# Attention, feed-forward and routed experts on one core: the first pass's weights converted two pieces a pair over six pairs, R's addition on GpSimd, M_prev in two buffers

## The chip, the core and the metric

The kernel runs on one core of one Trainium2 chip. The metric is device time in microseconds (us). The kernel before takes 1056.38 us (median of three runs, 1054.51 to 1058.94). The trace is of one further execution, which took 1052.92 us.

## The reference

Three layers follow one another. Attention: 4 batches, 8 heads, 576 positions, 64 wide; the causal softmax output is mixed, head by head, with a read from a memory `M_prev`. Feed-forward: 2304 tokens, 512 to 2048 to 512, squared ReLU. Routed experts: 8 experts, 288 tokens each, chosen greedily by sorted logits.

```python
a = np.exp(scores); a /= a.sum(-1, keepdims=True) + 1e-09
local = np.matmul(a, v)
mem_out = (phi(q) @ M_prev) / (phi(q) @ z_prev + 1e-6)
x = g * mem_out + (1 - g) * local          # g = sigmoid(beta)
h = np.maximum(x @ w_in, 0); x = (h * h) @ w_out
...
out[mask] = np.maximum(x[mask] @ w1[e], 0) @ w2[e]
```

`w_in` and `w_out` reach the kernel as 64-bit floats, read as pairs of 32-bit words; everything else is 32-bit.

## The kernel before

The program is attention with the first feed-forward pass woven in, then the rest of the feed-forward layer, then the experts. Only the first part is touched.

Attention works on 16 pairs of heads. `step(n)` runs from n = -2 to 16, and each step carries work of several pairs at once: it transposes the probabilities of pair n (`trans`), computes the scores of pair n+1 (`score`, `exponentials`), reads out pairs n and n-1 (`read`), and prepares the operands of pairs n+1 and n+2. A step has ten parts u; `fill` is called in each of them, at 20 counted places a step. TensorE's instructions stand in the order in which the code is written. On VectorE (DVE), ScalarE (ACT), GpSimd (POOL) and SyncE (SP, which issues the loads and stores), a scheduler sets the order when the program is built; each of these engines then works strictly through its list.

In `exponentials`, ScalarE's exponential leaves row sums in `R[:, 1]`. When it has done u = 3 and u = 8 of a pair's nine blocks of rows, VectorE adds 1e-9 (L243) and takes the reciprocal (L244), and GpSimd multiplies the probabilities `P` by it (L246). TensorE then transposes `P` (L271) and multiplies. That is 32 such additions over 128x4 or 128x5 values.

The feed-forward layer goes over the 16 chunks of the hidden dimension in three passes; the first pass takes chunks 0 to 5, and needs for each chunk a piece of `w_in` and a piece of `w_out`. `Ffn.weights` makes one piece: a load of 512 KB (`raw`, L428), then `narrow`, which rebuilds 32-bit floats from the 64-bit ones (ScalarE L36 writes `r`; VectorE L37, L38, L39 make `gf`), then `split` into two parts (ScalarE L25, GpSimd L26). In this text, a conversion is one such piece. Twelve conversions belong to the first pass. `fill` takes two from the list at every tenth counted place from step 0 on, `w_in` and `w_out` of a chunk in turn: four in each of steps 0, 1 and 2, as far as the scheduler keeps them there. From step 4 on (`n >= HP`), `fill` also weaves in the matmuls of the first pass (`Ffn.first`), about 60 a step.

`load_memory` brings a pair's `M_prev` into one buffer `mraw` and splits it; the next pair's load waits for that. At the start, `og9`, a table of the mixing weights, is built by twelve small copies on VectorE.

Of the kernel before, what the change touches and what calls it, by code (L numbers as in the profile page):

```python
# [29 lines left out]
def narrow(nc, f, tmp, raw):  # L30

    low, high = raw[..., 0], raw[..., 1]
    nc.scalar.activation(tmp.bitcast(F32), high.bitcast(F32), AF.Copy, scale=2.0 ** -112)  # L36
# [12 lines left out]
def attention(tc, ident, q, k, v, M_prev, z_prev, beta, x_d, fill, ended):  # L49
# [5 lines left out]
    with ExitStack() as ctx:  # L55
# [43 lines left out]
        og = one.tile([128, H], F32, name="og")  # L99
        nc.vector.tensor_scalar(og, g, -1.0, 1.0, op0=OP.mult, op1=OP.add)  # L100
        og9 = one.tile([128, HP, 9], F32, name="og9")
        for hp in range(HP):
            nc.vector.tensor_copy(og9[:, hp, 0:8].rearrange("p (t j) -> p t j", j=2),
                                  og[:, None, 2 * hp:2 * hp + 2].to_broadcast([128, 4, 2]))
            for j in range(2):
                nc.vector.tensor_copy(og9[64 * j:64 * j + 64, hp, 8:9],
                                      og[64 * j:64 * j + 64, 2 * hp + j:2 * hp + j + 1])
        qb = [one.tile([128, 2, 128], F32R, name=f"qb{i}") for i in range(2)]
        for t_ in qb:
            nc.vector.tensor_copy(t_.rearrange("p s c -> p (s c)"), maskw[:, 0:256])  # L110
# [6 lines left out]

        def load_memory(n):
            b, hp = divmod(n, HP)
            raw = one.tile([128, 2, 64], F32, name="mraw")  # L120
            for j in range(2):
                nc.sync.dma_start(raw[64 * j:64 * j + 64], M_prev[b, 2 * hp:2 * hp + 2].rearrange("h d e -> d h e"))
            m = MB[n] = two.tile([128, 2, 128], F32R, name="mb")
            split(nc, m[:, :, 0:64], m[:, :, 64:128], raw)
# [98 lines left out]
        def exponentials(n, u, ps):  # L223
# [16 lines left out]
            nc.scalar.activation(pw, pw, AF.Exp, bias=R[:, 0, u:u + 1], scale=-1.0, accum_out=R[:, 1, u:u + 1])  # L240
            if u in (3, 8):
                us = slice(0, 4) if u == 3 else slice(4, 9)
                nc.vector.tensor_scalar(R[:, 2, us], R[:, 1, us], 1e-9, None, op0=OP.add)  # L243
                nc.vector.reciprocal(R[:, 2, us], R[:, 2, us])  # L244
                for w in range(us.start, us.stop):
                    nc.gpsimd.tensor_scalar(PP[n][w], PP[n][w], R[:, 2, w:w + 1], og9[:, hp, w:w + 1],  # L246
                                            op0=OP.mult, op1=OP.mult)
# [145 lines left out]
class Ffn:  # L393
# [19 lines left out]
        nc.vector.tensor_tensor(self.two8, ident[0:16, 0:8], ident[0:16, 8:16], op=OP.add)  # L413
        self.win, self.wout, self.Y, self.have = {}, {}, {}, 0

    def weights(self, c, part, home, pool, eng, psum=None):

        nc = self.nc
        if part == 0:
            a = self.win[c] = home.tile([128, 2, KD, 128], F32R, name="win")  # L420
            dst = a.rearrange("p s k f -> p s (k f)")
            src = self.w_in[:, 256 * c:256 * c + 256].rearrange("(k p) f -> p k f", p=128)
        else:
            dst = self.wout[c] = home.tile([128, 2, DM], F32R, name="wout")
            src = self.w_out[128 * c:128 * c + 128].rearrange("p (k f) -> p k f", k=KD)
        first = pool is self.start
        raw = pool.tile([128, 2 * DM], I32, name=f"raw{part}" if first else "raw")
        nc.sync.dma_start(raw.rearrange("p (k f) -> p k f", k=KD), src)  # L428
        t_ = (psum or self.two).tile([128, DM], I32, name="pr" if psum and psum is self.p2x else "r")
        held = part and c >= PASSES[-1][0]  # L430
        f_ = (self.two if first else self.keep if held else pool).tile([128, DM], I32, name="gf")
        narrow(nc, f_, t_, raw.rearrange("p (n t) -> p n t", t=2))
        split(nc, dst[:, 0], dst[:, 1], f_.bitcast(F32), eng)
        if held:
            self.sums += [(f_, c - PASSES[-1][0], e) for e in range(8)]
        yield
# [713 lines left out]
def tile_attention_ffn_moe(ctx, tc, q, k, v, M_prev, z_prev, beta, w_in, w_out, w_gate, w1, w2, out):  # L1150
# [19 lines left out]
    def chunks(cs, home, pool, psum=None):  # L1170
        for c in cs:
            for part in range(2):
                yield from f.weights(c, part, home, pool, nc.gpsimd, psum)

    sctx = ExitStack()
    f.start = sctx.enter_context(tc.tile_pool(name="ffs", bufs=1, side="right"))
    conv, work = chunks(PASSES[0], wa, f.start), f.first(sctx.enter_context(tc.tile_pool(name="gfirst", bufs=8, side="right")))
    owed = [0, 0]

    def fill(n, c, place=True):  # L1180
        owed[1] += place
        if place and n >= 0 and owed[1] % 10 == 0:
            for _ in range(2):
                next(conv, None)
        owed[0] += c
        while n >= HP and owed[0] > 0:
            e = next(work, 0)
            if not e:
                break
            owed[0] -= e  # L1190
        owed[0] = min(owed[0], 0)
# [84 lines left out]
```

## Time and profile before

| what | us |
|---|---|
| median of three runs | 1056.38 (1054.51 to 1058.94) |
| profiled execution | 1052.92 |
| its span, first to last instruction | 1051.2 |
| attention with the first pass woven in | about 0 to 383 |
| steps 0 to 2 | 21.82 to 104.55 |
| steps 3 to 5 | 104.55 to 169.27 |
| steps 6 on | 169.27 to about 383 |

The steps are cut where TensorE begins the first scores of a pair (L217 on 128 columns). Read the table with the span: the times of stretches count from its start. The 1.7 us that the execution takes beyond its span lie around it.

### The profile page before, as it was taken

The numbers are of one execution on the slowest core, as the hardware profiler recorded it, in microseconds if no ns is written. First come the engines' busy times: TensorE is split into PE (matmuls) and PEld (weight loads), VectorE is DVE, ScalarE is ACT, GpSimd is POOL, SyncE is SP. The second block draws the span as 40 slices with busy tenths as digits, with TensorE's granted clock in tenths as the row PEclk, the third lists the DMA queues.
The fourth block names the chain that finished last, engine by engine and source line by source line (L and its number), as shares of the span: only waits on it lengthen the run. The fifth ranks groups of instructions, "written<-read, shape, count | busy, mean of one in ns | idle before, by whom it ended". The sixth has DMA issues, their size and how long they took to land.

```text
span 1051.2 us, 19788 instructions
## 1 busy us (share of the span) xinstructions
PE 959.6 (91%) x7017; PEld 879.5 (84%) x7017; DVE 666.5 (63%) x1966; ACT 553.2 (53%) x1370; POOL 528.1 (50%) x503
## 2 busy tenths in 40 slices
PE   5667789999999989999999999999598999999996
PEld 4455678988898989999999999977497888989996
DVE  6999878887888737456426952335775577674110
ACT  6676877988888746444322343431152443354531
POOL 3565666566765726334312111211294856687841
PEclk9677899999999999999999999999698999999998
DMA  6354455554645276769584232101541454447400
GB/s 151 103 152 122 95 155 141 125 160 98 174 107 142 68 235 215 226 215 307 196 289 152 86 128 98 61 22 39 203 161 62 168 183 148 153 136 254 150 27 27
DMA packets 150723, 150.75 MB, mean 143 GB/s; under 512 B 71640, under 2 KB 122840, under 8 KB 150496
## 3 DMA queue, kind: packets, MB, share of 16 engines
q1 hardware_dynamic: 147552, 140.05, 43.1%
q0 software_dynamic: 3072, 9.44, 2.9%
q8 instruction: 55, 0.90, 0.3%
q14 instruction: 44, 0.36, 0.1%
HBM read 111.69 MB, written 37.77 MB: 142 GB/s over the span
## 4 chain that ended last, share of the span: by engine, by line
PE 62%; DVE 13%; ACT 9%; issue 7%; DMA 4%; POOL 3%; SPq 2%; POOLq 0%; ACTq 0%; DVEq 0%
PE ph L1054 12%; PE ph L44 7%; PE ph L45 6%; PE ph L46 6%; PE py L44 4%; PE py L45 4%; PE py L46 4%; ACT P L240 3%; POOL wsp L1038 3%; PE ps L312 3%; PE ps L217 2%; PE rs L831 2%; PE ps L271 2%; DMA wraw<-in_moe_w_dram 1%; DVE ptb L26 1%
## 5 line engine op out<-in xcount | busy, mean ns | idle before, releaser
L477 POOL TENSOR_TENSOR gf<-r 128x384 f32<-128x384 f32 (+1 forms) x108 | 87.0, 807 | 205.7 <-ACT r L475 197.6
L1038 POOL TENSOR_TENSOR wsp<-wraw,wsp 128x1024 fp32r<-128x1024 f32 x64 | 151.0, 2393 | 41.5 <-ACT wsp L1036 41.2
L1054 PE MATMUL ph<-xs,wsp 128*128 128x288 f32 x768 | 121.3, 308 | 0.0
L26 DVE TENSOR_TENSOR gs<-gf,gs 128x384 fp32r<-128x384 f32 (+1 forms) x108 | 63.6, 589 | 90.7 <-ACT gs L25 90.4
L1054 PE MATMUL ph<-hs,wsp 128*128 128x288 f32 x768 | 115.9, 304 | 0.0
L246 POOL TENSOR_SCALAR P<-P,R,og 128x128 f32<-128x128 f32 (+2 forms) x144 | 95.4, 675 | 35.6 <-DVE R L244 15.3
L1054 PEld LDWEIGHTS ph<-xs,wsp 128*128 128x128 f32 x768 | 107.8, 194 | 3.5 <-issue 2.8
L1054 PEld LDWEIGHTS ph<-hs,wsp 128*128 128x128 f32 x768 | 105.7, 191 | 0.9 <-DVE hs L1078 0.4
L1036 ACT ACTIVATE wsp<-wraw 128x1024 fp32r<-128x1024 f32 x64 | 64.0, 1052 | 48.2 <-DMA wraw<-in_moe_w_dram 30.8
L475 ACT ACTIVATE r<-ph 128x384 f32<-128x384 f32 (+1 forms) x108 | 48.6, 450 | 75.5 <-PE ph L46 74.4
L240 ACT ACTIVATE P<-P,R 128x128 f32<-128x128 f32 (+2 forms) x144 | 83.3, 580 | 8.6 <-DVE R L228 4.2
L25 ACT ACTIVATE gs<-gf 128x384 fp32r<-128x384 f32 (+1 forms) x108 | 52.5, 486 | 56.3 <-POOL gf L477 48.0
L44 PE MATMUL ph<-xt,win 128*128 128x384 f32 x240 | 81.3, 339 | 0.0
L45 PE MATMUL ph<-xt,win 128*128 128x384 f32 x240 | 80.9, 337 | 0.0
L46 PE MATMUL ph<-xt,win 128*128 128x384 f32 x240 | 80.7, 336 | 0.0
L271 PE MATMUL ps<-ident,P 128*128 128x128 f32 x320 | 62.5, 303 | 13.9 <-DVE ptb L26 4.8
L44 PE MATMUL ph<-xs,win 128*128 128x288 f32 x192 | 63.5, 331 | 3.8 <-ACT yo L514 2.5
L217 PE MATMUL ps<-kt,qt 64*128 64x128 f32 (+3 forms) x384 | 56.3, 390 | 10.0 <-DVE kt L26 3.4
L45 PE MATMUL py<-gs,wout 128*128 128x384 f32 x192 | 64.6, 337 | 0.0
L26 DVE TENSOR_TENSOR ptb<-ps,ptb 128x256 fp32r<-128x256 f32 (+3 forms) x128 | 59.6, 467 | 6.9 <-ACT ptb L25 5.1
L46 PE MATMUL py<-gs,wout 128*128 128x384 f32 x192 | 63.9, 336 | 0.0
L228 DVE CUSTOM_DVE_ANT_0 P<-ps,maskw 128x128 f32<-128x128 f32 (+3 forms) x128 | 58.6, 483 | 7.6 <-PE ps L135 4.1
(259 smaller groups left out, 2612.9 us busy)
## 6 DMA issues: line engine op xcount, KB each, us to landing
wraw<-in_moe_w_dram SPq DMA_DIRECT2D x32, 1024.0 KB, 5.5
xt<-xs_d SPq DMA_DIRECT2D x12, 1536.0 KB, 7.2
x_d<-xo SPq DMA_DIRECT2D x32, 288.0 KB, 3.7
xf<-x_d SPq DMA_DIRECT2D x32, 288.0 KB, 3.7
xs_d<-xs SPq DMA_DIRECT2D x8, 1152.0 KB, 5.9
raw<-in_moe_w_in_dram SPq DMA_DIRECT2D x16, 512.0 KB, 4.8
raw<-in_moe_w_out_dram SPq DMA_DIRECT2D x16, 512.0 KB, 4.8
yp<-yo SPq DMA_DIRECT2D x32, 144.0 KB, 4.0
```

What stands on the lines that cost most here:

```text
L26: (eng or nc.vector).tensor_tensor(lo, src, hi.bitcast(F32), op=OP.subtract)
L44: nc.tensor.matmul(out, lhi, rhi, start=start, stop=False)
L45: nc.tensor.matmul(out, lhi, rlo, start=False, stop=False)
L46: nc.tensor.matmul(out, llo, rhi, start=False, stop=stop)
L217: nc.tensor.matmul(ps[j][:, 0:w], qt[r0, a, qs], kt[r0, b, 0:w], start=i == 0, stop=i == 2)
L240: nc.scalar.activation(pw, pw, AF.Exp, bias=R[:, 0, u:u + 1], scale=-1.0, accum_out=R[:, 1, u:u + 1])
L246: nc.gpsimd.tensor_scalar(PP[n][w], PP[n][w], R[:, 2, w:w + 1], og9[:, hp, w:w + 1], op0=OP.mult, op1=OP.mult)
L271: nc.tensor.transpose(tr[:, 128 * i:128 * i + 128], P[:, 128 * i:128 * i + 128], ident)
L477: nc.gpsimd.tensor_tensor(gf, r, r, op=OP.mult)
L1036: nc.scalar.activation(w[:, 0, hs], raw[:, hs], AF.Copy)
L1038: eng.tensor_tensor(w[:, 1, hs], raw[:, hs], w[:, 0, hs].bitcast(F32), op=OP.subtract)
L1054: nc.tensor.matmul(out, l[a], r[b], start=i + p == 0, stop=i == n - 1 and p == 2)
```

## The change

- The twelve conversions come in another order, all six of `w_in` first, then six of `w_out`, and at other places: one at each of two places in each of steps 0 to 5 (places 10 and 20; in step 5, places 4 and 10).
- `fetch` takes the load out of `weights`; the load of the next piece is issued at the place of the present one. Two buffers, raw0 and raw1, take turns (before there were two as well, one for `w_in` and one for `w_out`).
- These loads, and ScalarE's first operation of each conversion, are kept in the program's order, so the scheduler may not move them ahead.
- R's addition of 1e-9 (32 times) runs on GpSimd; the reciprocal stays on VectorE.
- `mraw` has two buffers; `og9` is built by three copies in place of twelve.

```diff
-        for hp in range(HP):
-            nc.vector.tensor_copy(og9[:, hp, 0:8].rearrange("p (t j) -> p t j", j=2),
-                                  og[:, None, 2 * hp:2 * hp + 2].to_broadcast([128, 4, 2]))
-            for j in range(2):
-                nc.vector.tensor_copy(og9[64 * j:64 * j + 64, hp, 8:9],
-                                      og[64 * j:64 * j + 64, 2 * hp + j:2 * hp + j + 1])
+        pairs = og.rearrange("p (h j) -> p h j", j=2)
+        nc.vector.tensor_copy(og9[:, :, 0:8].rearrange("p h (t j) -> p h t j", j=2),
+                              pairs[:, :, None, :].to_broadcast([128, HP, 4, 2]))
+        for j in range(2):
+            nc.vector.tensor_copy(og9[64 * j:64 * j + 64, :, 8], pairs[64 * j:64 * j + 64, :, j])
...
-            raw = one.tile([128, 2, 64], F32, name="mraw")
+            raw = two.tile([128, 2, 64], F32, name="mraw")
...
-                nc.vector.tensor_scalar(R[:, 2, us], R[:, 1, us], 1e-9, None, op0=OP.add)
+                nc.gpsimd.tensor_scalar(R[:, 2, us], R[:, 1, us], 1e-9, None, op0=OP.add)
...
+CONVERT = {0: (10, 0), 1: (10, 0), 2: (10, 0), 3: (10, 0), 4: (10, 0), 5: (4, 10)}
...
+    def fetch(self, c, part, pool, name="raw"):
+
+        raw = pool.tile([128, 2 * DM], I32, name=name)
...
+        a = self.nc.sync.dma_start(raw.rearrange("p (k f) -> p k f", k=KD), src)
+        if pool is self.start:
+            self.tc.keep_in_program_order(a)
+        return raw
...
-        narrow(nc, f_, t_, raw.rearrange("p (n t) -> p n t", t=2))
+        a = narrow(nc, f_, t_, raw.rearrange("p (n t) -> p n t", t=2))
+        if first:
+            self.tc.keep_in_program_order(a)
...
+    def apart(cs, home, pool):
+        todo = [(part, c) for part in range(2) for c in cs]
+        raws = []
+        for n, (part, c) in enumerate(todo):
+            for part_, c_ in todo[len(raws):n + 2]:
+                raws.append(f.fetch(c_, part_, pool, f"raw{len(raws) % 2}"))
+            yield from f.weights(c, part, home, pool, nc.gpsimd, None, raws[n])
...
-    conv, work = chunks(PASSES[0], wa, f.start), ...
+    conv, work = apart(PASSES[0], wa, f.start), ...
...
-        if place and n >= 0 and owed[1] % 10 == 0:
-            for _ in range(2):
-                next(conv, None)
+        if place and owed[1] % 20 in CONVERT.get(n, ()):
+            next(conv, None)
```

TensorE's order stays as it is, instruction for instruction; the other engines' orders differ as far as the end of attention. Below, three places (lines of the changed kernel are one or more higher: L107 is the old L106).

VectorE near the program's start, where the copies into og9 stand between the first pair's q side (qp) and its k (kt). Before:

```order
L176 SCALAR_TENSOR_TENSOR qp<-nq_175,e 128x640
L103 COPY og_205<-og 128x8
L106 COPY og_205<-og 64x1 x2
L103 COPY og_205<-og 128x8
L106 COPY og_205<-og 64x1 x2
L103 COPY og_205<-og 128x8
L106 COPY og_205<-og 64x1 x2
L103 COPY og_205<-og 128x8
L106 COPY og_205<-og 64x1 x2
L26 TENSOR_TENSOR kt<-ps,kt 128x512
```

With the change:

```order
L176 SCALAR_TENSOR_TENSOR qp<-nq_175,e 128x640
L104 COPY og_205<-og 128x4x8
L107 COPY og_205<-og 64x4 x2
L26 TENSOR_TENSOR kt<-ps,kt 128x512
```

Three copies stand ahead of kt in place of twelve.

VectorE in step 0, from the phi operation of a coming pair (L176) on; L37, L38 and L39 are a conversion's operations, L243 and L244 R's addition and reciprocal. Before:

```order
L176 SCALAR_TENSOR_TENSOR qp<-nq_176,e 128x640
L200 TENSOR_TENSOR qpt_426<-ps,qpt_426 64x512
L39 SCALAR_TENSOR_TENSOR gf<-raw_526,r 128x512
L26 TENSOR_TENSOR pta<-ps,pta 128x256
L244 RECIPROCAL R<-R 128x5
...
L37 TENSOR_SCALAR gf<-r 128x512
L200 TENSOR_TENSOR qpt_426<-ps,qpt_426 64x64
L243 TENSOR_SCALAR R<-R 128x4
L180 TENSOR_REDUCE nr<-e 128x10
L200 TENSOR_TENSOR qpt_427<-ps,qpt_427 64x512
L38 SCALAR_TENSOR_TENSOR r<-r,gf 128x512
```

With the change, from L176 on:

```order
L176 SCALAR_TENSOR_TENSOR qp<-nq_176,e 128x640
L200 TENSOR_TENSOR qpt_417<-ps,qpt_417 64x512
L26 TENSOR_TENSOR pta<-ps,pta 128x256 x2
L26 TENSOR_TENSOR qb_210<-ps,qb_210 64x64
L200 TENSOR_TENSOR qpt_417<-ps,qpt_417 64x64
L26 TENSOR_TENSOR ptb<-ps,ptb 128x3x128
L200 TENSOR_TENSOR qpt_418<-ps,qpt_418 64x512
L200 TENSOR_TENSOR qpt_418<-ps,qpt_418 64x64
L26 TENSOR_TENSOR qt<-ps,qt 128x512
L26 TENSOR_TENSOR kt<-ps,kt 128x512
L37 TENSOR_SCALAR gf<-r 128x512
```

The first conversion of the step begins only behind qt and kt; before, parts of two stand ahead of the reciprocal and among the qpt operations. The addition L243 is gone from this list.

VectorE in step 5, with the change, where before no conversion stood; gs is the feed-forward pass's hidden part, ptb the transposed probabilities:

```order
L184 TENSOR_TENSOR nr<-nr,g 128x10
L37 TENSOR_SCALAR gf<-r 128x512
L38 SCALAR_TENSOR_TENSOR r<-r,gf 128x512
L39 SCALAR_TENSOR_TENSOR gf<-raw_1800,r 128x512
L26 TENSOR_TENSOR gs<-gf,gs 128x288
L26 TENSOR_TENSOR qt<-ps,qt 128x512
L26 TENSOR_TENSOR gs<-gf,gs 128x288
L26 TENSOR_TENSOR kt<-ps,kt 128x512
L37 TENSOR_SCALAR gf<-r 128x512
L26 TENSOR_TENSOR ptb<-ps,ptb 128x3x128
```

A whole conversion stands ahead of gs, qt and kt, and the next one begins right behind them.

## Rows read from the trace of the kernel before

**Rows 1.** Windows by part: us, PE, PEld, DVE, ACT, POOL busy (count), PEclk, DMA share, GB/s

```profile
21.82:104.55 82.73, 56.43 (x288) 45.18 (x288) 77.23 (x198) 60.31 (x169) 48.09 (x48) 0.73 0.47 132
104.55:169.27 64.72, 55.66 (x380) 46.60 (x379) 54.64 (x172) 52.84 (x161) 40.47 (x48) 0.92 0.47 116
169.27:383.00 213.73, 208.47 (x1590) 190.00 (x1589) 172.20 (x526) 172.24 (x523) 130.15 (x157) 1.00 0.50 132
```

**Rows 2.** The same view, steps 2, 3, 4 and 5 one by one

```profile
78.25:104.55 26.30, 18.87 (x101) 14.95 (x100) 24.53 (x61) 18.64 (x53) 15.39 (x16) 0.77 0.43 122
104.55:125.43 20.88, 16.34 (x100) 12.66 (x99) 19.33 (x56) 15.89 (x48) 12.86 (x15) 0.84 0.39 90
125.43:147.95 22.52, 18.32 (x121) 15.14 (x120) 17.11 (x60) 17.96 (x56) 12.75 (x16) 0.92 0.61 163
147.95:169.27 21.32, 20.99 (x161) 18.80 (x160) 18.20 (x58) 18.99 (x59) 14.86 (x18) 1.00 0.39 93
```

**Rows 3.** Windows of VectorE's conversion operations (tile gf), steps 0, 1, 2

```profile
21.82:51.19 29.37, 12.40 (x15) 0.68 0.42 126
51.19:78.25 27.06, 10.57 (x14) 0.75 0.55 148
78.25:104.55 26.30, 8.02 (x9) 0.77 0.43 122
```

**Rows 4.** Tile gf up to 110 us: durations min/median/max in ns, starts

```profile
L37 DVE TENSOR_SCALAR gf<-r x12: 410/482/1727, 23.9 to 94.7; 128x512 int32<-128x512 int32 x12
L38 DVE SCALAR_TENSOR_TENSOR r<-r,gf x12: 673/690/1728, 26.3 to 98.4; 128x512 int32<-128x512 int32 x12
L39 DVE SCALAR_TENSOR_TENSOR gf<-raw,r x12: 675/754/1639, 28.9 to 101.8; 128x512 int32<-128x512 int32 x12
```

**Rows 5.** Windows of R's addition alone (L243, VectorE)

```profile
21.82:104.55 82.73, 4.29 (x6) 0.73 0.47 132
104.55:169.27 64.72, 4.72 (x7) 0.92 0.47 116
169.27:383.00 213.73, 7.02 (x18) 1.00 0.50 132
```

**Rows 6.** R's addition up to 400 us, its durations in ns

```profile
L243 DVE TENSOR_SCALAR R<-R x32: 154/221/2607, 17.6 to 360.5; 128x4 f32<-128x4 f32 x16, 128x5 f32<-128x5 f32 x16
```

**Rows 7.** Timeline of VectorE and TensorE: start, us, engine, line; in brackets idle before

```profile
112.09 2.61 DVE L243 TENSOR_SCALAR R<-R 128x4 f32<-128x4 f32 x1
178.92 1.14 DVE L243 TENSOR_SCALAR R<-R 128x4 f32<-128x4 f32 x1
180.57 0.79 PE L217 MATMUL ps<-kt,qt 64*128 64x384 f32 x6 [1.54 <-DVE ptb L26]
```

**Rows 8.** The same view of four engines at the program's start

```profile
9.39 0.16 DVE L103 COPY og<-og 128x8 f32<-128x8 f32 x1
9.69 1.53 POOL L177 TENSOR_TENSOR e<-qp,zb 128x640 f32<-128x640 f32 x1 [4.97 <-DMA zb<-in_z_prev_dram]
9.77 1.48 DVE L103 COPY og<-og 128x8 f32<-128x8 f32 x1
12.29 0.82 DVE L26 TENSOR_TENSOR kt<-ps,kt 128x512 fp32r<-128x512 f32 x2
13.03 1.43 PE L217 MATMUL ps<-kt,qt 64*128 64x128 f32 x10 [3.44 <-DVE kt L26]
13.87 0.74 ACT L172 ACTIVATE e<-nq 128x640 f32<-128x640 f32 x1 [0.51 <-DMA nq<-in_q_dram]
```

**Rows 9.** Groups by line and shape up to 383 us: busy us, mean ns, idle before

```profile
L36 ACT ACTIVATE r<-raw 128x512 f32<-128x512 f32 x12 | 8.0, 671 | 5.1 <-DMA raw<-in_moe_w_out_dram 2.9 <-DMA raw<-in_moe_w_in_dram 2.1
L246 POOL TENSOR_SCALAR P<-P,R,og 128x128 f32<-128x128 f32 x32 | 15.4, 489 | 8.6 <-DVE R L244 8.0 <-PE ph L46 0.7
L703 POOL IOTA j<- 128x3 f32 x1 | 0.1, 145 | 0.0
```

**Rows 10.** Waits of SP's queue up to 400 us: total us, times, longest

```profile
SPq L122 <- DVE mb L26: 66.0, 9, 14.1
```

More of the change, by code (lines that the diff above doesn't have):

```diff
@@ L35, in narrow @@
     low, high = raw[..., 0], raw[..., 1]
-    nc.scalar.activation(tmp.bitcast(F32), high.bitcast(F32), AF.Copy, scale=2.0 ** -112)
+    a = nc.scalar.activation(tmp.bitcast(F32), high.bitcast(F32), AF.Copy, scale=2.0 ** -112)
     nc.vector.tensor_scalar(f, tmp, 3, None, op0=OP.logical_shift_left)
@@ L39, in narrow @@
     nc.vector.scalar_tensor_tensor(f, low, 29, tmp, op0=OP.logical_shift_right, op1=OP.bitwise_or)
+    return a
 def mm3(nc, out, lhi, llo, rhi, rlo, start, stop):
@@ L414, in __init__, with weights @@
         self.win, self.wout, self.Y, self.have = {}, {}, {}, 0
-    def weights(self, c, part, home, pool, eng, psum=None):
+    def fetch(self, c, part, pool, name="raw"):
+        raw = pool.tile([128, 2 * DM], I32, name=name)
+        if part == 0:
+            src = self.w_in[:, 256 * c:256 * c + 256].rearrange("(k p) f -> p k f", p=128)
+        else:
+            src = self.w_out[128 * c:128 * c + 128].rearrange("p (k f) -> p k f", k=KD)
+        a = self.nc.sync.dma_start(raw.rearrange("p (k f) -> p k f", k=KD), src)
+        if pool is self.start:
+            self.tc.keep_in_program_order(a)
+        return raw
+    def weights(self, c, part, home, pool, eng, psum=None, raw=None):
         nc = self.nc
@@ L421, in weights @@
             dst = a.rearrange("p s k f -> p s (k f)")
-            src = self.w_in[:, 256 * c:256 * c + 256].rearrange("(k p) f -> p k f", p=128)
         else:
             dst = self.wout[c] = home.tile([128, 2, DM], F32R, name="wout")
-            src = self.w_out[128 * c:128 * c + 128].rearrange("p (k f) -> p k f", k=KD)
         first = pool is self.start
-        raw = pool.tile([128, 2 * DM], I32, name=f"raw{part}" if first else "raw")
-        nc.sync.dma_start(raw.rearrange("p (k f) -> p k f", k=KD), src)
+        raw = self.fetch(c, part, pool) if raw is None else raw
         t_ = (psum or self.two).tile([128, DM], I32, name="pr" if psum and psum is self.p2x else "r")
@@ L1173, in chunks @@
                 yield from f.weights(c, part, home, pool, nc.gpsimd, psum)
+    def apart(cs, home, pool):
[5 more added lines that the diff above has]
+            yield from f.weights(c, part, home, pool, nc.gpsimd, None, raws[n])
     sctx = ExitStack()
     f.start = sctx.enter_context(tc.tile_pool(name="ffs", bufs=1, side="right"))
-    conv, work = chunks(PASSES[0], wa, f.start), f.first(sctx.enter_context(tc.tile_pool(name="gfirst", bufs=8, side="right")))
+    conv, work = apart(PASSES[0], wa, f.start), f.first(sctx.enter_context(tc.tile_pool(name="gfirst", bufs=8, side="right")))
     owed = [0, 0]
```

## The prediction

> **What bounds the kernel now.** I read the windows first, cut where TensorE begins a new pair's first scores. In steps 0 to 2 TensorE is busy 56.43 of 82.73 us while VectorE is busy 77.23 us, 93% [rows 1]: VectorE sets the pace there. In steps 3 to 5 VectorE is busy 54.64 of 64.72 us (84%) and TensorE 55.66; from step 6 on TensorE is busy 208.47 of 213.73 us, so only 5.3 us can be won there [rows 1]. The granted clock goes with it: 0.73, 0.92, 1.00 of full speed, so between the levels of 1.2 and 2.4 GHz at first, after idle stretches of TensorE, and at 2.4 GHz from step 5 on [rows 1, 2]. So time can be won up to 169 us; what comes behind attention keeps its work and nearly its order, and I leave it as it is.
>
> Next I asked what fills VectorE in the early steps. Its conversion operations take 12.40, 10.57 and 8.02 us in steps 0, 1 and 2 [rows 3], together 30.99 us for twelve, or 2.58 us each. Undisturbed, one takes 0.410 + 0.673 + 0.675 = 1.76 us by the shortest of its three operations; the longest are 1.73, 1.73 and 1.64 us [rows 4]. Something holds them up. R's addition shows it more plainly: 4 or 5 values a partition take 154 ns at best and 2607 at worst [rows 6]. At 178.92 us one takes 1.14 us, and TensorE then waits 1.54 us for the transposed probabilities behind it [rows 7]. All 32 take 4.29 us in steps 0 to 2 (with 4.72 in steps 3 to 5 and 7.02 later) [rows 5].
>
> Why so long? The copy at 9.77 us takes 1.48 us where its like at 9.39 took 0.16, and GpSimd runs an operation from 9.69 to 11.22 [rows 8]: VectorE's copy ends with GpSimd's operation. The Trainium skill (SBUF — State Buffer, Who interferes with whom) says that certain VectorE operations from SBUF share a port pair with GpSimd, and that the loser of that lock waits for the whole other instruction. The trace agrees, with the 1.48 us.
>
> **The change, term by term.** The sums are made against the profiled 1052.92 us, which lies 3.5 us under the median of 1056.38; I apply the difference to the median.
>
> *Start.* Twelve copies fill VectorE from 9.39 to 12.29 us, and TensorE waits 3.44 us for the kt behind them [rows 8]. Three copies need some 0.5 us, so kt could go at 9.9: 2.4 us won. But ScalarE stands idle until 13.87 for its next e, by the trace for a load (which the change doesn't hasten), and its exponentials are queued behind that; the second or third copy may also still meet GpSimd's operation. Ends: 0 and -2.4; I take the middle, **-1.2**.
>
> *Steps 0 to 2, six conversions fewer and R's additions gone.* By VectorE's load: 77.23 - 30.99 / 2 - 4.29 = 57.4 us, plus the 5.5 us for which it is idle now, is 62.9: 19.8 us won. From the other side, by the nearest step without a conversion: step 3 takes 20.88 us, of which VectorE is busy 19.33 [rows 2]. R's addition in it takes at least the 2.61 us at 112.09 [rows 7]. So 20.88 - 2.61 + 2 x 2.58 = 23.4 us a step with two conversions, 70.3 for three: 12.4 won. Between them: **-16**. Loading a place earlier also removes ScalarE's waits on raw pieces, 5.1 us [rows 9]; I give it nothing, because VectorE is the busier engine throughout and covers it. Were VectorE not the bound, they would be part of the same gain.
>
> *Steps 3 to 5, six conversions more, R's additions gone.* VectorE's load becomes 54.64 - 4.72 + 6 x 2.58 = 65.4 us. If it can be filled to the 93% of the early steps, that needs 65.4 / 0.93 = 70.3 us: 5.6 lost. At the undisturbed 1.76 us it is 60.5 / 0.93 = 65.0: 0.3 lost. Step 4 has slack (17.11 of 22.52 us), step 5 has none on TensorE (20.99 of 21.32) [rows 2]. There a conversion stands whole ahead of gs, qt and kt, and TensorE waits for these. I take **+3.5**, nearer the upper end, as GpSimd is busy 40.47 of 64.72 us here, 63%, against 48.09 of 82.73, 58%, in steps 0 to 2 [rows 1], so the price should not fall.
>
> *Steps 6 on.* R's addition frees 7.02 us of VectorE [rows 5], but TensorE is idle only 5.3 us in all, and 1.5 of it is the wait of rows 7. Ends 0 and -2.5; I take **-1**.
>
> *R's addition on GpSimd.* No row shows GpSimd adding on four columns. From below the index list of three columns, 0.145 us; from above the 128-column multiplication, 0.489 us [rows 9], so 4.6 to 15.6 us on an engine that is busy 48% to 63% of the time: hidden, save in the chain exponential, addition, reciprocal, multiplication, where VectorE's 0.154 is replaced. Thirteen of them lie in the steps up to 5 [rows 5]; at up to 0.34 more each that is 0 to 4.4 us. I take **+1**. Behind a waiting addition stand the multiplications of the same probabilities, which would wait anyway, and at times a feed-forward operation.
>
> *M_prev twice.* SP's queue stands 66.0 us, in nine waits, behind the one mraw [rows 10]; but it loads a pair ahead, and TensorE names no such load in its waits. **0**, with perhaps 1 us won; if the cover were gone, one late load would cost the longest wait, 14.1 us.
>
> Sum: -1.2 - 16 + 3.5 - 1 + 1 = **-13.7 us**, 1039.2 for an execution like the profiled one, **1042.7** against the median.
>
> **The rivals.**
>
> *The late steps pay it back* (0.18). In steps 3 to 5 each conversion meets GpSimd at work in each of its three operations. At the longest of rows 4 one costs 5.09 us; half-way between that and the mean, 3.8 us, six cost 23, VectorE's load is 72.7 and the stretch 78.2 us: +13.5 in place of +3.5, so -3.7 in all, 1052.7. For it: step 5's full TensorE [rows 2]. Against it: in steps 0 to 2, with three operations a conversion, the counts give 2.3 to 2.7 us each [rows 3]. The lock of which the Trainium skill tells (the same page and section) would lead here: by it the price hangs on how often the two engines meet.
>
> *More than the middle* (0.20). VectorE's load decides, and the clock rises earlier because TensorE is less often idle: -19.8 in steps 0 to 2, +0.3 in steps 3 to 5, -2.4 at the start, the rest as above: -21.9, 1034.5. For it: 93% in the early steps. Against it: other chains (ScalarE is busy 60.31 of 82.73 us [rows 1]) should show as VectorE clears.
>
> *Slower: ScalarE waits at the pinned places* (0.07). The loads of raw and L36 can no longer be moved by the scheduler. If SP's queue stands (it does for 14.1 us at worst [rows 10]) when a raw load's turn comes, L36 waits on ScalarE, and behind it all exponentials. At the longest of today's kind of wait, 2.5 us for each of twelve, and with nothing hidden, this costs 30 us: +16, 1072.7. From 13.7 / 12 = 1.1 us a conversion on the kernel is slower than before. Against it: the load is issued ten places, about half a step, ahead, and the M_prev that held SP's queue now has a second buffer.
>
> **How the numbers follow.** The forecast holds 0.55, the rivals 0.18, 0.20 and 0.07. Ends of the terms together: -2.4 - 19.8 + 0.3 - 2.5 + 0 = -24.4, so 1032.0; 0 - 12.4 + 5.6 + 0 + 4.4 = -2.4, so 1054.0. The second rival lies inside, the first just inside; I give 1032 to 1054 for 8 in 10. A measurement of this kernel can tell about 0.5%, 5.3 us, from no change: faster means under 1051.1. Forecast and second rival are nearly all faster, of the first rival about a quarter: 0.79. No change 0.14, slower 0.07.
>
> **What would show it.** Right: in the profile after, steps 0 to 2 take 64 to 69 us, with VectorE's conversion operations near 5 us a step; steps 3 to 5 take 66 to 70 us; no VectorE addition stretches beyond 1 us, and GpSimd's take 0.15 to 0.5. Wrong: steps 3 to 5 above 75 us with TensorE waiting on gs, kt or ptb; early steps that stay above 75 us with VectorE well under 90%; ScalarE idle before L36 on loads for more than 1 us each.

## The result, and the profile after

The changed kernel takes 1045.81 us in the median of 19 runs (1039.13 to 1053.63), the kernel before 1056.02 on the same chip: a ratio of 0.9912, 95% interval 0.9891 to 0.9933, so 9.3 us faster (the ratio is not that of the medians, which differ by 10.2). The profiled execution took 1049.03 us with a span of 1047.3. Forecast were 1042.7 us and 13.7 us of gain.

The windows of the profile after, cut as in [rows 1], with the same columns:

```profile
19.78:86.33 66.55, 50.92 (x287) 40.35 (x287) 59.40 (x173) 53.74 (x160) 42.74 (x49) 0.77 0.51 132
86.33:161.05 74.72, 57.98 (x378) 48.80 (x379) 65.78 (x183) 59.27 (x173) 53.54 (x60) 0.86 0.51 136
161.05:374.00 212.95, 209.46 (x1590) 190.57 (x1589) 170.03 (x509) 172.46 (x524) 136.04 (x176) 1.00 0.50 132
```

Steps 0 to 2 fall from 82.73 to 66.55 us, steps 3 to 5 rise from 64.72 to 74.72. VectorE's idle time in the second stretch is 74.72 - 65.78 = 8.9 us. Steps 3, 4 and 5 one by one, to be read beside [rows 2]:

```profile
86.33:107.36 21.03, 16.80 (x99) 13.27 (x99) 20.01 (x58) 17.61 (x52) 15.20 (x18) 0.84 0.49 140
107.36:131.90 24.54, 18.78 (x121) 15.41 (x121) 21.47 (x61) 19.57 (x60) 19.63 (x23) 0.86 0.71 192
131.90:161.05 29.15, 22.40 (x159) 20.13 (x160) 24.30 (x66) 22.08 (x63) 18.71 (x21) 0.88 0.35 85
```

Step 5 alone is 7.8 us longer: TensorE's idle time in it has grown from 0.33 to 6.75 us, its busy time from 20.99 to 22.40, and its granted clock has fallen from 1.00 to 0.88. TensorE's waits in steps 4 and 5 (line, releaser: us, times, longest) and the same place on ScalarE (timeline: start, us, idle before in brackets) show where:

```profile
PE ph L45 <- ACT r L487: 6.6, 1, 6.6
```

```profile
142.44 0.74 ACT L172 ACTIVATE e<-nq 128x640 f32<-128x640 f32 x1 [2.24 <-DVE nr L180]
143.20 0.74 ACT L173 ACTIVATE e<-e 128x640 f32<-128x640 f32 x1
143.84 0.65 ACT L36 ACTIVATE r<-raw 128x512 f32<-128x512 f32 x1
144.51 0.41 ACT L487 ACTIVATE r<-ph 128x288 f32<-128x288 f32 x1
```

The ReLU (L487) for which TensorE waits stands behind the pinned conversion (L36), and that behind the feature map's two operations (L172, L173), the first of which waits for VectorE. What VectorE does for conversions (tile gf), for [rows 3], and the durations of its three operations and of R's addition, for [rows 4, 6]:

```profile
19.78:41.20 21.42, 1.80 (x3) 0.70 0.48 121
41.20:64.55 23.35, 4.55 (x6) 0.83 0.46 129
64.55:86.33 21.78, 3.59 (x6) 0.76 0.60 147
```

```profile
L37 DVE TENSOR_SCALAR gf<-r x12: 387/457/970, 30.8 to 150.1; 128x512 int32<-128x512 int32 x12
L38 DVE SCALAR_TENSOR_TENSOR r<-r,gf x12: 674/688/1279, 34.0 to 150.9; 128x512 int32<-128x512 int32 x12
L39 DVE SCALAR_TENSOR_TENSOR gf<-raw,r x12: 677/686/1112, 37.5 to 152.8; 128x512 int32<-128x512 int32 x12
L243 POOL TENSOR_SCALAR R<-R x32: 222/242/896, 15.6 to 351.4; 128x4 f32<-128x4 f32 x16, 128x5 f32<-128x5 f32 x16
```

Each conversion has three of these operations, so VectorE does 15 of the 36, five conversions' worth and not six, in steps 0 to 2; the other seven conversions follow in steps 3 to 5. The longest operations shrink from 1.73, 1.73 and 1.64 us to 0.97, 1.28 and 1.11. ScalarE no longer waits for a raw piece before L36 (5.1 us in [rows 9]). The start, for [rows 8]: three copies take the place of twelve, kt is 2.4 us sooner and TensorE waits 0.99 us in place of 3.44.

```profile
9.41 0.17 DVE L104 COPY og<-og 128x32 f32<-128x32 f32 x1
9.50 0.34 DVE L107 COPY og<-og 64x4 f32<-64x4 f32 x2
9.86 0.82 DVE L26 TENSOR_TENSOR kt<-ps,kt 128x512 fp32r<-128x512 f32 x2
10.61 1.44 PE L217 MATMUL ps<-kt,qt 64*128 64x128 f32 x10 [0.99 <-DVE kt L26]
```

SyncE's queue up to 400 us stands less behind mraw than in [rows 10]:

```profile
SPq L122 <- DVE mb L26: 40.1, 6, 9.4
```

Attention's last matmul (L309) starts at 368.61 us, against 377.69 before.

### The profile page after: what moved, and what is told of

Read it like the earlier page. It is cut to its first block, busy times and chain, and to the rows that moved or that the text cites. A ratio compares the mean times of both kernels' runs of the same rounds, so it can differ in the third digit from the quotient of the medians.

```text
span 1047.3 us, 19732 instructions
## 1 busy us (share of the span) xinstructions
PE 959.4 (92%) x7017; PEld 879.1 (84%) x7017; DVE 655.2 (63%) x1925; ACT 552.6 (53%) x1370; POOL 540.3 (52%) x535
## 4 chain that ended last, share of the span: by engine, by line
PE 61%; DVE 12%; issue 7%; DMA 6%; ACT 6%; POOL 5%; SPq 1%; POOLq 0%; DVEq 0%; ACTq 0%
PE ph L1066 12%; PE ph L45 6%; PE ph L46 6%; PE ph L47 6%; PE py L45 4%; PE py L46 4%; PE py L47 4%; PE ps L312 3%; POOL wsp L1050 3%; PE ps L217 3%; PE ps L271 2%; PE rs L843 2%; DMA raw<-in_moe_w_out_dram 1%; DMA raw<-in_moe_w_in_dram 1%; ACT P L240 1%
## 5 line engine op out<-in xcount | busy, mean ns | idle before, releaser
L246 POOL TENSOR_SCALAR P<-P,R,og 128x128 f32<-128x128 f32 (+2 forms) x144 | 99.5, 707 | 24.6 <-DVE R L244 17.7
L487 ACT ACTIVATE r<-ph 128x384 f32<-128x384 f32 (+1 forms) x108 | 48.6, 450 | 77.6 <-PE ph L47 76.5
L46 PE MATMUL py<-gs,wout 128*128 128x384 f32 x192 | 64.7, 338 | 0.3 <-DVE gs L26 0.3
L47 PE MATMUL py<-gs,wout 128*128 128x384 f32 x192 | 63.9, 336 | 0.0
L26 DVE TENSOR_TENSOR ptb<-ps,ptb 128x384 fp32r<-128x384 f32 (+3 forms) x128 | 59.1, 464 | 7.4 <-ACT ptb L25 5.8
L45 PE MATMUL py<-gs,wout 128*128 128x384 f32 x192 | 63.4, 338 | 0.0
```

The costliest lines, as they stand in the source:

```text
L26: (eng or nc.vector).tensor_tensor(lo, src, hi.bitcast(F32), op=OP.subtract)
L45: nc.tensor.matmul(out, lhi, rhi, start=start, stop=False)
L46: nc.tensor.matmul(out, lhi, rlo, start=False, stop=False)
L47: nc.tensor.matmul(out, llo, rhi, start=False, stop=stop)
```

## The experiments

All kernels below are the changed one with an edit, or unaltered (e8), but for e7, which is the kernel before with one. Kernels of one group ran on one chip; the kernel before had medians of 1054.2, 1066.2, 1054.2 and 1065.9 us in the four groups, so times are compared by ratio, and marks within attention directly, which the chip hardly moves (e8 ends attention at 368.36 us, after at 368.61, on chips whose times differ by 1%). The table has, for each profile, the windows cut as above. Two of its kernels, e8 and e11, have the same order as the changed kernel on TensorE, VectorE, ScalarE and GpSimd; the other edits gave the scheduler an order of their own. What these three profiles differ by is therefore the least that a difference must exceed to be read: 138.95 to 142.00 us for the six steps, 29.13 to 29.31 for step 5, 207.5 to 209.6 from step 6 to the last L309.

| kernel | ratio to before (95%) | steps 0-2, us | steps 3-5 | step 5 | six steps | VectorE busy in them | L309 last |
|---|---|---|---|---|---|---|---|
| before | 1 | 82.73 | 64.72 | 21.32 | 147.45 | 131.87 | 377.69 |
| after | 0.9912 (0.9891-0.9933) | 66.55 | 74.72 | 29.15 | 141.27 | 125.18 | 368.61 |
| e1 no pin | 0.9967 (0.9946-0.9987) | 74.83 | 69.99 | 26.47 | 144.82 | 128.94 | 374.43 |
| e2 early | 0.9932 (0.9910-0.9954) | 69.19 | 73.18 | 24.26 | 142.37 | 124.25 | 370.80 |
| e3 burst | 0.9999 (0.9974-1.0024) | 80.00 | 69.03 | 24.88 | 149.03 | 132.13 | 376.75 |
| e4 addition on VectorE | 0.9959 (0.9932-0.9986) | 67.82 | 78.14 | 29.87 | 145.96 | 127.35 | 372.87 |
| e5 place 3 | 0.9947 (0.9919-0.9976) | 67.63 | 73.69 | 28.57 | 141.32 | 126.68 | 371.94 |
| e6 old copies | 0.9989 (0.9971-1.0007) | 65.49 | 79.53 | 31.18 | 145.02 | 123.69 | 375.17 |
| e7 before + addition | 1.0015 (0.9991-1.0039) | 82.78 | 63.05 | 23.26 | 145.83 | 128.84 | 376.55 |
| e8 again | 0.9914 (0.9885-0.9944) | 64.50 | 74.45 | 29.13 | 138.95 | 123.70 | 368.36 |
| e9 no sign | 0.9988 (0.9966-1.0010) | 68.22 | 76.28 | 31.84 | 144.50 | 117.08 | 373.93 |
| e10 no addition | 0.9921 (0.9891-0.9951) | 66.89 | 79.53 | 29.06 | 146.42 | 121.00 | 370.70 |
| e11 one mraw | 0.9922 (0.9893-0.9950) | 67.28 | 74.72 | 29.31 | 142.00 | 124.96 | 369.22 |
| e12 no VectorE | 0.9967 (0.9941-0.9993) | 64.39 | 78.10 | 29.10 | 142.49 | 101.78 | 375.38 |

### The places and the pin (e1 to e3)

e1 takes the pin away:

```diff
-        if first:
-            self.tc.keep_in_program_order(a)
```

> The changed kernel, but ScalarE's first operation of each conversion may be moved by the scheduler again (the loads stay in the program's order). In step 5 the ReLU of the second hidden chunk then stands ahead of phi's e and of the conversion. Theory A (step 5 is long, 29.15 us, because that ReLU waits behind e and a pinned conversion): step 5 falls to 22 to 24 us, no wait of TensorE above 2 us on a ReLU there. Theory B (step 5 is long because VectorE has two more conversions to do): step 5 stays at 27 to 30 us. In either case steps 0 to 2 may get longer, as the scheduler pulls conversions together again: if they go from 66.6 to over 75 us, the pinning is what makes the early gain.

Windows of steps 0 to 2 and 3 to 5:

```profile
19.80:94.63 74.83, 56.84 (x288) 44.77 (x288) 68.70 (x185) 58.02 (x162) 50.41 (x53) 0.73 0.55 146
94.63:164.62 69.99, 57.87 (x379) 48.53 (x379) 60.24 (x173) 56.41 (x170) 46.75 (x58) 0.91 0.46 118
```

Without the pin the scheduler pulls nine of the twelve conversions back into steps 0 to 2 (ScalarE's L36 at 22.53 to 69.32 us, the next at 133.65) and 3.5 us of the gain go, more than half of the six steps' 6.2. So the pin does the spreading; the places in the table alone don't. Step 5, with one conversion left in it, takes 26.47 us, between the ranges of the two theories.

e2 gives step 5 none and steps 2 and 3 one more each:

```diff
-CONVERT = {0: (10, 0), 1: (10, 0), 2: (10, 0), 3: (10, 0), 4: (10, 0), 5: (4, 10)}
+CONVERT = {0: (10, 0), 1: (10, 0), 2: (7, 14, 0), 3: (7, 14, 0), 4: (10, 0)}
```

> The changed kernel with the last two conversions taken out of step 5: two each in steps 0 and 1, three each in steps 2 and 3, two in step 4, all pinned. Theory A and B both say that step 5 falls to 21 to 23 us. Steps 2 and 3 show the price of one more conversion where TensorE is not full: if VectorE sets the pace there, 2 to 2.6 us each, 24 and 23.5 us in place of 21.8 and 21.0; if a chain of waits does, under 1 us each. Attention ends 2 to 6 us earlier than in the changed kernel (368.6 us); the whole is 0 to 5 us faster than it.

Step 5 falls from 29.15 to 24.26 us and the ReLU's wait is gone, but steps 2 and 3 rise to 24.74 and 25.67 (21.78 and 21.03 after): the six steps take 142.37 us, just above the three profiles of equal order, and the ratio can't be told from that of after. The conversions' price moved with them, and at 3.0 and 4.6 us it is above the 2 to 2.6 that was expected of VectorE's load.

e3 puts all twelve, pinned, into steps 0 to 2:

```diff
-CONVERT = {0: (10, 0), 1: (10, 0), 2: (10, 0), 3: (10, 0), 4: (10, 0), 5: (4, 10)}
+CONVERT = {0: (5, 10, 15, 0), 1: (5, 10, 15, 0), 2: (5, 10, 15, 0)}
```

> The changed kernel with the twelve conversions back in steps 0 to 2, four a step at places 5, 10, 15 and 20, pinned and loaded a place early. If spreading them over six steps makes the early gain (VectorE's load): steps 0 to 2 take 79 to 84 us against 66.6, steps 3 to 5 take 60 to 63. If the loads ahead of time and the pinned places make it, steps 0 to 2 stay under 72 us, and with short steps 3 to 5 this is the fastest version, attention ending near 358 us.

Steps 0 to 2 are back at 80.00 us and the whole gain is gone, at a granted clock of 0.64 in them (six of VectorE's conversion operations, 6.17 us, still slip into step 3, and steps 3 to 5 take 69.03 us, not 60 to 63): it is the spreading over six steps that gains, not the new order of pieces, not the early loads and not the pin as such.

### Step 5's wait (e5)

One number changes, so that the conversion stands ahead of the feature map:

```diff
-CONVERT = {0: (10, 0), 1: (10, 0), 2: (10, 0), 3: (10, 0), 4: (10, 0), 5: (4, 10)}
+CONVERT = {0: (10, 0), 1: (10, 0), 2: (10, 0), 3: (10, 0), 4: (10, 0), 5: (3, 10)}
```

> The changed kernel with one number changed: the first conversion of step 5 is pinned at place 3 instead of 4, that is ahead of the next pair's feature map in program order, so that on ScalarE the ReLU of the hidden chunk is no longer held behind it and behind the exponential part of that map. Theory (the 6.6 us wait of TensorE for the ReLU is the price of the pinned place): that wait is under 1 us, step 5 takes 22 to 24.5 us instead of 29.2, the steps before it are as in the changed kernel to 1 us, attention ends at 362 to 365 us instead of 368.6 and the time is 1039 to 1043 us, a ratio of 0.983 to 0.988 to the kernel before. Rival (step 5 is long since two conversions and the hidden chunks fill VectorE, busy for 24.3 of 29.2 us, and the ReLU is only where it shows): step 5 stays at 27 us or more with a new wait of 4 us or more, on VectorE's part of the hidden chunk or on the exponentials, and the time is 1044 to 1048 us, 0.990 to 0.993.

The wait for the ReLU is gone, yet step 5 takes 28.57 us. In that the rival came true; of its new wait of 4 us or more there is none, the longest of TensorE's waits in the step is

```profile
PE ps L131 <- issue: 1.9, 1, 1.9
```

Attention ends 3.3 us later than after, all of it behind the six steps, which take the same time. Window of step 5, and VectorE's timeline where the idle time now hides (its first conversion operation is stretched to 1.82 us; from there to 152.55 the timeline shows no idle time):

```profile
132.56:161.13 28.57, 24.18 (x160) 21.02 (x160) 26.21 (x65) 22.44 (x63) 18.80 (x22) 0.88 0.37 92
```

```profile
137.97 1.82 DVE L37 TENSOR_SCALAR gf<-r 128x512 int32<-128x512 int32 x1 [0.68 <-ACT r L36]
139.82 0.68 DVE L200 TENSOR_TENSOR qpt<-ps,qpt 64x512 fp32r<-64x512 f32 x1
140.54 0.69 DVE L38 SCALAR_TENSOR_TENSOR r<-r,gf 128x512 int32<-128x512 int32 x1
...
142.55 1.58 DVE L39 SCALAR_TENSOR_TENSOR gf<-raw,r 128x512 int32<-128x512 int32 x1
```

Of the 7.25 us by which this step 5 is longer than that of before, TensorE's own work makes 3.19 (24.18 us busy for 20.99, at a granted clock of 0.88 for 1.00) and idle stretches 4.06; in after it was 1.41 and 6.42. So taking the 6.6 us away did not give them back: other waits and the clock took their place. In nine of ten profiles at hand the six steps' length was VectorE's busy time plus 14.6 to 18.6 us (in e6 it was 21.3), and I formed the theory that VectorE's load bounds them; e9 and e12 are its test.

### VectorE's load (e9, e12)

e9, in the first pass's conversions only:

```diff
-    nc.vector.scalar_tensor_tensor(tmp, tmp, -2 ** 31, f, op0=OP.bitwise_and, op1=OP.bitwise_or)
-    nc.vector.scalar_tensor_tensor(f, low, 29, tmp, op0=OP.logical_shift_right, op1=OP.bitwise_or)
+    if not first:
+        nc.vector.scalar_tensor_tensor(tmp, tmp, -2 ** 31, f, op0=OP.bitwise_and, op1=OP.bitwise_or)
+    nc.vector.scalar_tensor_tensor(f, low, 29, f if first else tmp, op0=OP.logical_shift_right, op1=OP.bitwise_or)
```

> The changed kernel without the second of VectorE's three operations of a conversion, the one that puts the sign back, in the twelve conversions of the first pass alone; these weights lose their sign, all else is computed. Theory (VectorE bounds the six steps: in nine profiles their length is VectorE's busy time in them plus 14.6 to 18.6 us, whatever order or places were chosen): twelve operations of 0.69 to 0.76 us go, busy time falls from 124 to 125 us to 115 to 117, and the six steps take 131 to 134 us instead of 139 to 141; the time is 0.980 to 0.985 of the kernel before. Rival (the pinned places on ScalarE, or TensorE's clock with 108 us of matmuls, set the length): the steps take 137 us or more, and the ratio is 0.988 to 0.992.

VectorE's busy time falls by 8.1 us, to 117.08; the six steps get 3.2 us longer, 144.50 us where the theory asked for 131 to 134. In step 5 TensorE again waits for the ReLU:

```profile
132.44:164.28 31.84, 25.14 (x159) 22.53 (x159) 23.29 (x63) 23.83 (x70) 18.74 (x23) 0.84 0.32 77
```

```profile
PE ph L46 <- ACT r L488: 5.6, 1, 5.6
```

e12 leaves out all three of VectorE's operations in these conversions:

```diff
     a = nc.scalar.activation(tmp.bitcast(F32), high.bitcast(F32), AF.Copy, scale=2.0 ** -112)
+    if first:
+        return a
...
-        f_ = (self.two if first else self.keep if held else pool).tile([128, DM], I32, name="gf")
+        f_ = t_ if first else (self.keep if held else pool).tile([128, DM], I32, name="gf")
```

> The changed kernel without any of VectorE's three operations in the twelve conversions of the first pass: their result is taken as ScalarE's operation leaves it, so these weights are wrong; the loads, ScalarE's pinned operation, and the splitting on ScalarE and GpSimd stay, and so does the order on ScalarE (feature map, pinned conversion, ReLU) in step 5. It takes 28.5 us off VectorE's busy time in the six steps. Theory (a conversion's price is VectorE's time, in step 5 too): the six steps take 118 to 128 us instead of 139 to 142, of which step 5 25.5 us or less, and the ratio to the kernel before is 0.970 to 0.980. Rival 1 (in step 5 it is the order on ScalarE behind GpSimd's queue, elsewhere VectorE): steps 0 to 4 fall from 110 to 112 us to 103 or less, but step 5 stays at 28 to 31 us with the ReLU's wait at 5 us or more; the ratio is 0.978 to 0.984. Rival 2 (VectorE's work is hidden, and the pinned places and the splitting on GpSimd make the length, as when the sign's operation went and nothing was won): the six steps take 137 us or more, the ratio is 0.988 or more.

By its numbers rival 2 came true. With 23.4 us less on VectorE the six steps take 142.49 us. Its windows of steps 0 to 2 and 3 to 5, its waits of TensorE in step 5, and of GpSimd over the six steps:

```profile
19.77:84.16 64.39, 50.41 (x287) 40.32 (x287) 50.07 (x161) 53.81 (x161) 41.38 (x52) 0.85 0.55 137
84.16:162.26 78.10, 60.58 (x380) 51.51 (x379) 51.71 (x158) 59.45 (x172) 47.10 (x57) 0.84 0.49 132
```

```profile
PE ph L47 <- ACT r L489: 6.0, 1, 6.0
```

```profile
POOL xf L476 <- DMA xf<-x_d: 12.6, 4, 4.0
```

VectorE is idle for 40.7 of 142.49 us, and nothing is won. e9 and e12 have orders of their own as well, but a new order that costs 5 us, the most seen below, would not hide the 11 us or more that the theory asked of e12. At the changed kernel's load VectorE's work is therefore not what bounds these steps; that its busy time went with their length before would fit if both came from the same stretching, which no run tests. What bounds them is open: GpSimd waits 12.6 us for pieces of x, which is 4.6 us in after, and no run moves those loads.

### R's addition (e4, e7, e10)

e4 puts it back on VectorE in the changed kernel, e7 moves it to GpSimd in the kernel before, e10 drops it:

```diff
-                nc.gpsimd.tensor_scalar(R[:, 2, us], R[:, 1, us], 1e-9, None, op0=OP.add)
-                nc.vector.reciprocal(R[:, 2, us], R[:, 2, us])
+                nc.vector.reciprocal(R[:, 2, us], R[:, 1, us])
```

> The changed kernel with R's addition back on VectorE. If the additions on VectorE cost what they take there (9.0 us up to step 5, against GpSimd's 0.1 to 0.5 us each): steps 0 to 5 are 4 to 9 us longer than the changed kernel's 141.3. If their long times were only waits that something else would have filled: within 2 us. The whole follows by the same amount, 1047 to 1055 us.

> The kernel before with only R's addition on GpSimd, and all else as it was. Theory (VectorE's additions took 9.0 us in steps 0 to 5 since each stretched while GpSimd was busy, and the path to the next scores paid part of it; putting the addition back on VectorE in the changed kernel cost 4.7 us of those steps): steps 0 to 5 take 142 to 145 us instead of 147.5, the time is 1050 to 1053 us, a ratio of 0.995 to 0.998. Rival (in the kernel before the end of each step is set by other waits, and the 4.7 us came from another order of the scheduler): steps 0 to 5 take 146.5 to 148.5 us and the ratio is 0.998 to 1.002.

> The changed kernel without R's addition of 1e-9 on either engine: the reciprocal reads the sums directly. The sums hold exp(0) = 1, so that the addition changes no bit of them. Theory (VectorE bounds the six steps, the addition is no longer on it, and GpSimd's 0.24 us is hidden): VectorE's busy time stays at 122.5 to 126 us, the six steps take 138.5 to 142 us, the ratio is 0.989 to 0.993 as in the changed kernel. Rival (the hop from ScalarE over GpSimd to VectorE holds up the normalization and with it the turned P blocks): the reciprocal follows the exponential by over 0.5 us sooner, TensorE's waits on P and the ring shrink, the steps are shorter by 2 us or more and the ratio is 0.984 to 0.988.

In e7, 9.0 us of stretched additions leave VectorE in steps 0 to 5 [rows 5], its busy time there falls by only 3.0 us, and the time does not change; the six steps, 145.83 us, lie between the theory's range and the rival's. Groups by line and shape in those steps (busy us, mean ns), first of the kernel before, then of e7:

```profile
L176 DVE SCALAR_TENSOR_TENSOR qp<-nq,e 128x640 f32<-128x640 f32 x6 | 5.2, 862 | 0.0
L26 DVE TENSOR_TENSOR gs<-gf,gs 128x288 fp32r<-128x288 f32 x6 | 3.0, 495 | 0.2 <-ACT gs L25 0.2
L239 DVE TENSOR_TENSOR R<-R 128x1 f32<-128x1 f32 x7 | 1.4, 198 | 0.0
```

```profile
L176 DVE SCALAR_TENSOR_TENSOR qp<-nq,e 128x640 f32<-128x640 f32 x6 | 6.9, 1144 | 0.0
L236 DVE CUSTOM_DVE_ANT_0 P<-ps,maskt 128x288 f32<-128x288 f32 x14 | 6.1, 446 | 0.0
L26 DVE TENSOR_TENSOR gs<-gf,gs 128x288 fp32r<-128x288 f32 x6 | 4.9, 815 | 0.2 <-ACT gs L25 0.2
L239 DVE TENSOR_TENSOR R<-R 128x1 f32<-128x1 f32 x7 | 2.4, 336 | 0.1
```

So these operations are longer by part of what left. That the hold-up itself passed on to them fits, but e7's order differs from that of before too, and the two aren't separated. In e4 the six steps grow by 4.7 us with the addition on VectorE; in e10 they grow by 5.2 us with no addition at all, so e4's growth can't be put down to the addition. Behind step 5 e10 gains: from its step 6 to the last L309 it takes 204.4 us, where the equal orders take 207.5 to 209.6. The two cancel, and the ratio is that of after.

### The old copies, mraw, and the kernel once more (e6, e11, e8)

e6 puts the loop of twelve copies back (the first hunk of the diff on og9, reversed), e11 one buffer (`two` back to `one` for mraw), e8 alters nothing.

> The changed kernel with the twelve small copies of the gate's table, one part of the change, put back. Theory (they hold up VectorE's first key copy by about 2 us, as the start before and after differ): TensorE's second part of the first scores waits for the key copy by 3 to 3.5 us instead of 1.0, step 0 begins at 21.5 to 22 us instead of 19.8, and all that follows is later by 1.5 to 2.5 us: attention ends at 370 to 371 us, the time is 1047 to 1049 us, a ratio of 0.992 to 0.995. Rival (the start is made up within the first steps, whose length other engines set): step 0 begins 2 us later, but attention ends within 0.7 us of the changed kernel's 368.6, and the time is 1045 to 1047 us.

> The changed kernel with one buffer for the raw M_prev, as the kernel before had. Theory (the second buffer is worth nothing, the first term of the forecast that was set at 0): the ratio is 0.989 to 0.993, attention ends within 2 us of the changed kernel's two profiles (368.4 and 368.6 us). Rival (the load of the next M_prev waits in SyncE's queue for the buffer and holds up the raw weights that are now loaded a place early): ScalarE waits for raw weights for over 1 us somewhere in steps 0 to 5, attention ends at 371 us or later, and the ratio is 0.993 or more.

> The changed kernel once more, nothing altered, to see what of its profile belongs to the program and what to one execution. Theory (its loss in step 5 and its loss behind attention are the program's own): every step is within 0.7 us of the first profile, step 5 is 28 to 30 us with the ReLU's wait at 6 to 7 us, attention ends at 368 to 369.5 us, and from its last matmul to the first of the later passes it takes 65.5 to 67.5 us, as in the first profile. Rival (the loss behind attention, 66.5 against 62.3 us in the kernel before, is one execution's clock): steps as above, but that stretch takes 62 to 64 us. The ratio to the kernel before is 0.988 to 0.993 in either case.

In e6 the wait for kt is back, and step 0 begins at 21.88 us, 2.1 later:

```profile
13.07 1.43 PE L218 MATMUL ps<-kt,qt 64*128 64x128 f32 x10 [3.49 <-DVE kt L26]
```

But attention ends 6.6 us later, not 2.1: steps 3 to 5 have become 79.53 us. Nine tiny copies at the start can't cost that 80 us later by their work. The built programs' orders may: compared without buffer numbers, TensorE's order is the same in after, e6, e9, e10 and e11, while in each of e6, e9 and e10 over 100 of VectorE's 1925 instructions and 75 or more of ScalarE's 1226 stand elsewhere or are gone. The scheduler laid out the other engines afresh. In e8 and e11, where no instruction of VectorE, ScalarE or GpSimd stands elsewhere, steps 3 to 5 are 74.45 and 74.72 us (after 74.72), the ratios 0.9914 and 0.9922. Windows of steps 3 to 5, of e6 and of e8:

```profile
87.37:166.90 79.53, 63.65 (x379) 54.81 (x378) 66.57 (x180) 60.49 (x173) 51.43 (x59) 0.79 0.48 127
84.28:158.73 74.45, 58.18 (x378) 49.29 (x378) 65.59 (x183) 59.58 (x174) 53.75 (x60) 0.86 0.52 136
```

That the order makes the 5 us is thus the likeliest cause, but not shown: no run has the old copies under the order of after.

e8 also tells about the stretch behind attention. From the last L309 to the first matmul on xt the profile after took 66.35 us, against 62.33 before; e8 takes 63.80 and e11 63.53, with the same order. So most of those 4 us were that one execution, whose granted clock there was 0.97 against 1.00 in the other three.

For e11 SyncE's queue stands 51.8 us behind mraw (40.1 after), without an effect that these runs can tell.

## Why the prediction was right, and where it was not

The time came out 3.1 us above the forecast, inside its range; by the ratio the gain is 4.4 us short. Of its signs, steps 0 to 2 came out right (66.55 us) and steps 3 to 5 wrong (74.72 us for 66 to 70), with TensorE's long wait on a ReLU, not on gs, kt or ptb; GpSimd's longest addition took 0.90 us for at most 0.5. By its terms:

- *Start, -1.2.* Measured -2.0 (step 0 begins at 19.78, not 21.82 us), near the far end. e6 shows that the copies are the cause. ScalarE's wait for its load, which I set against it, was not on the path.
- *Steps 0 to 2, -16.* Measured -16.2, in e8 -18.2 and in e11 -15.5. e3 shows that the spreading does it. But the reason, that VectorE's load sets the pace, holds at most for the 93% of before. The load that I worked out, 57.4 us, came out at 59.40, and near it only by luck: five conversions, 9.94 us, took the place of the 15.5 reckoned for six, while VectorE's other work grew from 77.23 - 30.99 - 4.29 = 41.95 us to 59.40 - 9.94 = 49.46. Taking operations away did not leave the rest as it was. The stretch that I reckoned from the load without a drawback, 62.9, came out at 66.55; and in e12 the load is 50.07 us and the stretch 64.39. In the profiles with 50 to 60 us of load the stretch takes 64 to 69 us whatever the load, so there other waits among the engines hold it. That the middle between the load and the nearest step without a conversion met the measured number is luck too.
- *Steps 3 to 5, +3.5.* Measured +10.0, in e8 +9.7: this is the term that was mis-sized, and with 6.5 us it is more than the whole miss. Its load came out at 65.78 us busy for the 65.4 forecast, but with seven conversions at 2.3 us for six at 2.58. The step that failed was to divide it by 0.93, as though VectorE could again be filled as in the early steps: it is filled to 88%, and the +10.0 lies 4.4 us beyond even the upper end, 5.6, of this term. Of the 10.0 us, 7.8 lie in step 5. There every profile with two conversions takes 28.6 to 31.8 us, that with one 26.47 (e1), and those with none pinned there 21.3 to 24.9 (before, e2, e3, e7; the last one of e2 begins 0.2 us ahead of the step). Neither of the two causes that I tried explains this alone: without the ReLU's wait the step is 28.57 us (e5), without VectorE's part 29.10 (e12). But e12 has the ReLU's wait, 6.0 us, and e5 has VectorE's part; no run takes both away at once, so that each holds the step when the other is gone is not ruled out. What stays of a conversion in both is ScalarE's two operations, GpSimd's subtraction of 1.3 us, and the order around them. Which of all these makes the step long is open; a conversion in step 5 without GpSimd's subtraction was not tried either.
- *Steps 6 on, -1.* Measured 207.6 against 208.4 us to the last L309: -0.9. With the same order e11 takes 207.5 us and e8 209.6, so a gain of this size can't be told from none.
- *R's addition on GpSimd, +1.* It takes 242 ns in the median, within the bounds of 0.145 and 0.489. On the kernel before it is worth nothing that can be measured (e7), and its price inside the other terms is not to be had apart, since e4 and e10 changed the order as well. Unforeseen: from step 6 on e10 gains 3.1 us over after, with another order as well; none of my bounds asked about dropping the addition.
- *M_prev twice, 0.* e11: 0.9922 against 0.9912 and 0.9914. Right.

The measured terms give -2.0 - 16.2 + 10.0 - 0.9 = -9.1 us up to the last L309, and the ratio -9.3.

Of the rivals, *the late steps pay it back* was the nearest in kind: three quarters of its +13.5 came, though not by its mechanism. A conversion did not cost 3.8 us of VectorE: tile gf's operations take 28.7 us in steps 0 to 5, of which 2.9 are six subtractions for gs, and the rest is 2.1 us for each of twelve, less than the 2.58 of before. *More than the middle* rested on VectorE's load and a clock that rises earlier. The load is not the bound, and the clock rose only from 0.73 to 0.77 in steps 0 to 2 and fell from 1.00 to 0.88 in step 5. ScalarE did wait at a pinned place, as the *slower* rival has it, but not for a load and for 2.24 us once.

## What to carry to other kernels

A busy share of 93% says which engine to relieve first, but not how far: find the length at which the next limit takes over by leaving that engine's work out, before dividing a load by a share. Nearly every edit under a scheduler draws a new order of the engines that it may arrange. Here two that should have cost little (e6, e10) came with such a draw and with six steps that were 3.8 and 5.2 us longer, where three profiles of one order spread over 3.1 us; so repeat the unaltered kernel, compare the orders of the built programs, and credit to an edit without reserve only what an equal order shows. Where work is pinned for spreading, look at what may no longer pass it on the same engine.

## What the runs showed of the hardware that was not expected

Taking held-up operations off VectorE did not take their time off it. In e7, 9.0 us of additions left and VectorE's busy time fell by 3.0, while operations beside them grew, the one-column minimum L239 from 198 to 336 ns in the mean. In the changed kernel, where the additions are gone as well, it takes 648 ns in the mean of the six steps:

```profile
L236 DVE CUSTOM_DVE_ANT_0 P<-ps,maskt 128x288 f32<-128x288 f32 x14 | 6.1, 448 | 0.1
L239 DVE TENSOR_TENSOR R<-R 128x1 f32<-128x1 f32 x7 | 4.5, 648 | 0.1
L26 DVE TENSOR_TENSOR xs<-xf,xs 128x288 fp32r<-128x288 f32 x6 | 3.8, 649 | 0.0
```

That number is of one execution: by the same view L239 takes 394 ns in e8 and 504 in e11, and 524 in e4, where the additions are back on VectorE. So the additions' leaving can't be all that lengthens it.

Beside it the score operation L236, with 288 columns and one operand in PSUM, takes 448 ns, as before and in e7 (448 and 446): in the profiles of before, after, e4, e7 and e8, up to 400 us, only operations whose operands all lie in SBUF are stretched by over 0.15 us. The Trainium skill (SBUF — State Buffer, Who interferes with whom) says so too: a VectorE instruction with at most one SBUF input outside the two-port modes doesn't contend with GpSimd, and one with two SBUF inputs does, when GpSimd's reads SBUF. These rows agree. What they add is that VectorE's busy time fell by a third of what was moved away; that the hold-up went on to the next operation that can be caught fits, and isn't shown apart from the new order.
